# A gated attention unit followed by an MLP mixer: z^T without copies, w_tok2 in its own order, the first u^T on TensorE, x of batch 0 turned later

## The chip, the cores and the metric

One core of one Trainium2 chip runs the whole kernel in one launch. The metric is the time of one execution on the device in microseconds (us), as the median of several runs. TensorE (PE) multiplies, VectorE (DVE) and ScalarE (ACT) work element by element, GpSimd (POOL) copies and issues the casting loads, SyncE (SP) issues the transposing DMAs and the stores. Each engine runs its own instructions in the order in which they were written.

## The reference

There are 8 batches of 3008 rows, 256 channels wide, and z has 64 columns.

```
scores = (z @ z.T) / S;  attn = max(scores, 0) ** 2     # per batch, S = 3008
x  = u * (attn @ v)                                     # 3008 x 256
h  = max(x.T @ w_tok1, 0) @ w_tok2                      # 256 x 3008
u2 = x + h.T
out = u2 + max(u2 @ w_ch1, 0) @ w_ch2
```

w_tok1 is 3008 x 256, w_tok2 256 x 3008, w_ch1 256 x 1536, w_ch2 1536 x 256. All inputs and the output are float32; the kernel multiplies in bf16.

## The kernel before

**Tiles.** Rows of a batch are 24 tiles of 128, the last half full. Four tiles make a group, so a batch has six query blocks q and six key groups g. Rows are loaded so that a partition holds consecutive rows (`rows_of`, L102): within a group, tile t holds rows t, t+4, t+8 and so on. Everything made from z, u and v stands in that order, and w_tok2's columns have to be brought into it.

**Attention.** Scores (L399) multiply z^T with itself over 64 rows, so two key tiles share the array, one on its upper and one on its lower rows. For that zT holds z^T twice, on partitions 0 to 63 and 64 to 127. ScalarE applies max(., 0) out of PSUM into `at` (L437), VectorE squares it (L445), and TensorE multiplies by v into two accumulators (L533). `at` has six buffers. For batches 1 to 7 the score matrix's symmetry is used: a block above the diagonal is turned by a transposing DMA into the block below it (`flip`, L492), and diagonal blocks are filled in the same way (`flip_tiles`, L485). A buffer of `at` that is flipped comes free only when the flip has landed. The first batch computes every block. A finished accumulator is multiplied by u^T (`gate`, L628), which gives x^T; SP turns it into x (`turn_x`, L640).

**Mixer.** When all six blocks of a batch have x, token mixing (L675, L692) and the two channel matmuls (L729, L771) run between the attention work of the next batch. `add` (L698) adds the token-mixed h out of PSUM to x^T.

**z.** For a later batch GpSimd loads a group of z with a cast (`load_z`, L113), copies it twice side by side (`turn_z`, L125), and SP transposes that into four tiles of zT (L126), six times a batch. For batch 0 z is loaded uncast; VectorE doubles and casts it, TensorE turns chunks 0, 1, 4 and 5, and SP turns 2 and 3.

**u.** A block of u is loaded by GpSimd (L179) into one of three buffers and turned by SP (`turn_u`, L189). **w_tok2** is loaded into a staging tile `ws` (L208) and brought into row order by GpSimd copies (L220, L224).

**Order.** The program is written out by a planner (L1000 onwards) that keeps a clock for TensorE, ScalarE, VectorE and SP with fixed costs (`push`), and picks the next piece for TensorE: scores, a half of attn @ v, or a piece of the mixer. Loads and turns are asked for at fixed steps (`at_group`), a step being one key group of one block; batch 0 takes steps 0 to 35. In batch 0 GpSimd's queue loads v of batch 1, w_tok1, w_tok2 and the channel weights from step 7 on. The planner's costs decide only the order; on the chip each engine waits for what it needs.

Of the kernel before, what the change touches and what calls it, by code (L numbers as in the profile page):

```python
# [15 lines left out]
GK = 4  # L16
# [28 lines left out]
class Piece:  # L45


    def __init__(self, cost, needs, fn, opens=False, closes=False, room=None):
        self.cost, self.needs, self.fn = cost, needs, fn
        self.opens, self.closes, self.room = opens, closes, room  # L50


@with_exitstack
def kernel(
# [23 lines left out]
    NG = KT // GK  # L78
    widths = [min(QW, S - q * QW) for q in range(NQ)]
# [15 lines left out]


# [13 lines left out]
    def load_z(b, c):  # L110
        zs = sb.tile([P, GK, d_qk], BF16, tag="zs", name="zs", bufs=6)
        n = full_tiles[c]
        nc.gpsimd.dma_start(out=zs[:, :n, :], in_=rows_of(z[b], c))  # L113
        if n < GK:
            for r in range(2):
                nc.gpsimd.dma_start(
                    out=zs[r * TAIL:(r + 1) * TAIL, n, :], in_=last_rows(z[b]))
        loading(LOAD / 4)
        return zs

    def turn_z(zs, zT, c, engine, tag="zr", bufs=2):


        zr = sb.tile([P, GK, 2, d_qk], BF16, tag=tag, name="zr", bufs=bufs)
        engine.tensor_copy(zr[:], zs.unsqueeze(2).to_broadcast([P, GK, 2, d_qk]))  # L125
        nc.sync.dma_start_transpose(  # L126
            out=zT[:, c * GK:c * GK + GK, :], in_=zr.rearrange("p t h d -> p (t h d)"))
# [77 lines left out]
    def load_w_tok2(c):  # L205
        st = sb.tile([P, DT, QW], BF16, tag="h2", name="ws", bufs=ROOM["h2"])
        W = widths[c]
        nc.gpsimd.dma_start(  # L208
            out=st[:, :, :W],
            in_=moe_w_tok2.rearrange("(tc t) s -> t tc s", t=P)[:, :, c * QW:c * QW + W])  # L210
        ws[c] = st
        live["h2"] += 1
        loading(LOAD)

    def order_w_tok2(c):
        st = ws.pop(c)
        live["h2"] -= 1
        W, n = widths[c], full_tiles[c]
        for h in range(DT):
            nc.gpsimd.tensor_copy(  # L220
                w_tok2_sb[:, h, c * QW:c * QW + n * P].rearrange("p (t s) -> p t s", s=P),
                st[:, h, :n * P].rearrange("p (s t) -> p t s", t=n))
        if n * P < W:
            nc.gpsimd.tensor_copy(  # L224
                w_tok2_sb[:, :, c * QW + n * P:c * QW + W], st[:, :, n * P:W])
# [16 lines left out]
    zTs, vs, urs, uTs, xTs, xs, ws = {}, {}, {}, {}, {}, {}, {}  # L242
# [9 lines left out]

    LAST = NG - 1
# [41 lines left out]

    LOAD = 1.3
# [84 lines left out]
    def score_run(us, start):  # L381
        slots = sorted((d for d in ring if d.t is not None), key=lambda d: d.t)
        for unit in us:
# [12 lines left out]
            for r, i, c0, c1 in parts(unit):  # L396
                k = g * GK + i
                h = slice(r * d_qk, (r + 1) * d_qk)
                nc.tensor.matmul(  # L399
                    sc[:, r, c0:c1], zT[h, k * P:(k + 1) * P],  # L400
                    zT[h, q * QW + c0:q * QW + c1], start=True, stop=True)
# [41 lines left out]
    def square(unit, view, t):  # L443
        (b, q, g), pr = unit
        nc.vector.tensor_mul(view, view, view)  # L445
        if (b, q, g) in early:
            for e in early[b, q, g][2 * pr:2 * pr + 2]:
                e.t = t
            if pr == 0:
                blocks[b, q, g] = (  # L450
                    Done(t), ats[b, q, g].rearrange("p (i w) -> p i w", w=QW), "at", [1])
            else:
                ats.pop((b, q, g))
            return
        if pr < GK // 2 - 1:
            return
        at = ats.pop((b, q, g))
        uses = [1]
        if flips(b, q, g):
            uses[0] = 2  # L460
            attn = at.rearrange("p (j i s) -> p i j s", i=GK, s=P)
            done = push("sp", t, 2.45, 6.5, lambda t: flip(b, q, g, at, uses, done),
                        room=("fl",))
        else:
            attn = at.rearrange("p (i w) -> p i w", w=QW)
        blocks[b, q, g] = (Done(t), attn, "at", uses)

    def square_triangle(unit, t):
# [5 lines left out]
        if pr == 0:  # L474
            for j, busy in ((0, 0.55), (1, 0.4)):
# [3 lines left out]
        done = push("sp", t, 0.3, 5.5, lambda t: blocks.update(  # L479
# [136 lines left out]
    def gate(blk, dh, t):  # L616
# [18 lines left out]
        if dh == DT - 1:  # L635
            push("sp", t, 1.25, 7.5, lambda t: turn_x(b, q, t), first=1)
# [22 lines left out]
    def add_mixer(b):  # L659
# [26 lines left out]
        def tok2(q, end):  # L686
# [9 lines left out]
            def add(t):  # L696
                xT = xTs[b, q]
                nc.vector.tensor_add(xT[:, :, :W], xT[:, :, :W], h[:, :, :W])  # L698
# [187 lines left out]
    def new_zT(b):  # L886
        zTs[b] = sb.tile([P, KT, P], BF16, tag="zT", name="zT", bufs=2)
# [7 lines left out]
    load_v(0, 0)  # L895

# [10 lines left out]
    def turn_next_z(b, c, zs):  # L907
        turn_z(zs, zTs[b + 1], c, nc.gpsimd)
        on_sp(0.6)
        turned[b + 1, c] = Done(pe[0] + 9.0)  # L910
# [7 lines left out]
    for b in range(B):  # L918
# [6 lines left out]
        if b + 1 < B:  # L925
            held = {}

            def ask_z(b, c, held):
                held[c] = load_z(b + 1, c)

            at_group(base + 3 * NG, lambda b=b: new_zT(b + 1))
            for j, c in enumerate(vorder):
                at_group(base + 3 * NG + j, lambda b=b, c=c, h=held: ask_z(b, c, h))
                at_group(base + 3 * NG + j + 3, lambda b=b, c=c, h=held:
                         turn_next_z(b, c, h.pop(c)))
# [3 lines left out]
    def turn_late_z(c):  # L939


        zr = double_first_z(c)
        free["dve"] = max(free["dve"], pe[0]) + 0.45
        while all(d.t is None for d in ring):
            run_engines(next_op()[0][0])
        begin = max(free["dve"] + 0.1, min(d.t for d in ring if d.t is not None))
        take_slot()
        begin, end = on_pe(max(pe[0], begin), "full", 0.23)
        zp = psum.tile([P, GK, P], F32, tag="ps", name="zp", bufs=3)
        turn_on_pe(zr, zp)  # L950
        turned[0, c] = Done()
        ring.append(push(
            "dve", end + 0.1, 0.66, 0.8,
            lambda t: nc.vector.tensor_copy(zTs[0][:, c * GK:c * GK + GK, :], zp[:]),
            first=1, done=turned[0, c]))

    for c in range(GK, NG):
        at_group(c - GK + 1, lambda c=c: turn_late_z(c))
    at_group(3, lambda: turn_u(0, 0))
# [10 lines left out]
    first_tok2 = len(items)  # L970
    items += [lambda c=c: load_w_tok2(c) for c in range(NG)]
    items += [lambda part=part: ask_w_ch(part) for part in range(4)]
    for k, item in enumerate(items):
        n = NG + 1 + k * (NQ * NG - 2 * NG + 4) // len(items)
        at_group(n, item)
        if 0 <= k - first_tok2 < NG:
            at_group(n + 4, lambda c=k - first_tok2: order_w_tok2(c))
# [9 lines left out]
    for c in range(DT, GK):  # L987
        turn_z(zf0[c], zTs[0], c, nc.vector, "h2", 8)
# [5 lines left out]
    score_run(units[:2], 5.3)  # L994

# [4 lines left out]
    while cur[0] is not None or heads or tails:  # L1000
# [32 lines left out]
        if n_now and ts <= t + NOW and (whole or (low and n_now >= 2)):  # L1033
            pick = "scores"
        elif (starved and now and can_score(done_units, now) == now
              and has_turned(units[done_units:done_units + now]) <= t + NOW):
            pick, n_now, ts = "scores", now, t
        elif hold and opened[0] is not None and tm <= t + NOW and pieces is opened[0]:
# [36 lines left out]
        else:  # L1075
            budget -= pieces[0].cost
# [34 lines left out]
```

## Time and profile before

| what | value |
|---|---|
| median of 4 runs | 1177.43 us (1170.79 to 1182.73) |
| the profiled execution | 1178.86 us, span 1176.9 us |
| TensorE matmul busy | 1157.4 us, 98% of the span |
| VectorE, ScalarE, GpSimd busy | 541.0, 521.4, 159.7 us |
| transposes and stores (hardware queue) | 131.74 MB |
| casting loads (software queue) | 32.32 MB written |
| zr copies, GpSimd (L125) | 42, 26.3 us |
| w_tok2 copies, GpSimd (L220, L224) | 13, 10.5 us |
| mean granted TensorE clock | 0.996 |

A line of the profile names the source line, the engine, the operation and its tiles, and then how often and how long. "Idle before" is how long the engine stood before such instructions and what ended it. In the page's rows of 40 digits each digit is a slice of 29.4 us.

### The profile page before, as it was taken

How to read it: one execution, taken by the hardware profiler on the slowest of the kernel's cores; microseconds unless marked ns; L12 is line 12 of the kernel's file. 1: busy time of each engine (PE TensorE's matmuls, PEld its weight loads, DVE VectorE, ACT ScalarE, POOL GpSimd, SP SyncE). 2: the span in 40 equal slices, each digit the busy share in tenths (PEclk: the TensorE clock that was granted, in tenths of full speed). 3: DMA queues.
4: the chain of work that ended last, by engine and by line, in shares of the span. 5: the costliest groups of instructions: out<-in, count | busy, mean ns of one | idle time of the engine just before them, and what ended most of it. 6: DMA issues, size and time to landing. Idle time of an engine off the chain costs nothing.

```text
span 1176.9 us, 17698 instructions
## 1 busy us (share of the span) xinstructions
PE 1157.4 (98%) x6956; PEld 631.2 (54%) x7049; DVE 541.0 (46%) x819; ACT 521.4 (44%) x650; POOL 159.7 (14%) x328
## 2 busy tenths in 40 slices
PE   9997999999999999999999999999999999999998
PEld 3333455655556555465555555555554655555666
DVE  5784652436523464335634354242542436512544
ACT  7885542343633354333533436345353445513221
POOL 4471001002011200110201210011101010000000
PEclk9998999999999999999999999999999999999999
DMA  9999837896578984886859896697676977532121
GB/s 169 184 134 193 160 85 156 167 179 122 134 149 165 170 144 114 161 167 148 156 111 184 154 159 130 126 195 139 126 141 146 192 136 155 124 94 63 50 81 64
DMA packets 472883, 165.57 MB, mean 141 GB/s; under 512 B 436640, under 2 KB 450528, under 8 KB 472800
## 3 DMA queue, kind: packets, MB, share of 16 engines
q1 hardware_dynamic: 444944, 131.74, 53.5%
q0 software_dynamic: 27344, 32.32, 19.5%
q8 instruction: 55, 0.90, 0.3%
q10 hardware_dynamic: 512, 0.38, 0.1%
q14 instruction: 28, 0.23, 0.1%
HBM read 65.40 MB, written 24.64 MB: 77 GB/s over the span
## 4 chain that ended last, share of the span: by engine, by line
PE 95%; DMA 2%; issue 1%; ACT 1%; DVE 1%; SPq 0%; POOL 0%; ACTq 0%; DVEq 0%
PE acc L533 41%; PE op L771 21%; PE hp L729 21%; PE sc L399 6%; PE a_ps L675 4%; PE h_ps L692 3%; DMA fl<-at 1%; ACT at L437 1%; DMA zf<-in_z_dram 1%; DMA v_sb<-in_v_dram 0%; DVE xT L698 0%; DVE at L445 0%; DVE xT L628 0%; DVE h2pre L744 0%; SPq L134 0%
## 5 line engine op out<-in xcount | busy, mean ns | idle before, releaser
L742 ACT ACTIVATE h2pre<-hp 128x1024 bf16<-128x1024 f32 (+1 forms) x191 | 191.0, 1006 | 364.6 <-PE hp L729 363.4
L533 PEld LDWEIGHTS <-v_sb 128*128 128x128 bf16 (+1 forms) x2304 | 209.5, 98 | 266.4 <-issue 65.0
L533 PE MATMUL acc<-at,v_sb 128*128 128x512 bf16 (+2 forms) x1438 | 348.0, 378 | 3.0 <-issue 1.3
L437 ACT ACTIVATE at<-sc 128x1024 bf16<-128x1024 f32 (+1 forms) x284 | 272.0, 1024 | 165.6 <-PE sc L399 155.1
L445 DVE TENSOR_TENSOR at<-at 128x1024 bf16<-128x1024 bf16 (+1 forms) x284 | 199.8, 712 | 183.7 <-ACT at L437 182.8
L729 PE MATMUL hp<-xT,w_ch_sb 128*128 128x512 bf16 (+1 forms) x1115 | 264.8, 374 | 1.9
L771 PE MATMUL op<-w_ch_sb,h2pre 128*128 128x256 bf16 x2208 | 258.4, 273 | 0.3 <-DVE xT L698 0.2
L771 PEld LDWEIGHTS <-h2pre 128*128 128x128 bf16 x2208 | 216.0, 98 | 46.1 <-issue 0.5
L533 PE MATMUL acc<-fl,v_sb 128*128 128x512 bf16 (+1 forms) x819 | 197.6, 370 | 1.4 <-issue 0.5
L729 PEld LDWEIGHTS <-w_ch_sb 128*128 128x128 bf16 x1152 | 112.8, 98 | 126.7 <-issue 0.2
L784 DVE TENSOR_TENSOR res<-op,u_sb 128x512 f32<-128x512 f32 x87 | 60.2, 692 | 206.5 <-PE op L771 206.5
L744 DVE TENSOR_SCALAR h2pre<-hp 128x1024 bf16<-128x1024 f32 (+1 forms) x97 | 117.3, 1209 | 52.4 <-PE hp L729 51.3
L628 DVE TENSOR_TENSOR xT<-acc,uT 128x512 bf16<-128x512 f32 (+1 forms) x96 | 63.3, 665 | 113.7 <-PE acc L533 110.4
L399 PE MATMUL sc<-zT 64*128 64x512 bf16 (+1 forms) x732 | 96.0, 362 | 0.3
L425 ACT ACTIVATE at<-sc 128x512 bf16<-128x512 f32 (+3 forms) x164 | 59.2, 446 | 67.7 <-PE sc L399 67.5
L125 POOL COPY zr<-zs 128x512 bf16<-128x512 bf16 x42 | 26.3, 625 | 401.3 <-DMA zT<-zr 396.3
L473 DVE TENSOR_TENSOR at<-at 128x512 bf16<-128x512 bf16 (+3 forms) x164 | 44.3, 324 | 59.2 <-ACT at L425 59.1
L399 PEld LDWEIGHTS <-zT 64*128 64x128 bf16 x732 | 31.3, 94 | 56.9 <-issue 39.6
L698 DVE TENSOR_TENSOR xT<-xT,h_ps 128x1024 bf16<-128x1024 bf16 (+1 forms) x48 | 55.7, 1193 | 6.4 <-PE h_ps L692 6.3
L675 PE MATMUL a_ps<-x_sb,w_tok_sb 128*128 128x256 bf16 x384 | 47.5, 283 | 5.8 <-ACT at L437 5.8
L675 PEld LDWEIGHTS <-w_tok_sb 128*128 128x128 bf16 x384 | 38.8, 101 | 15.6 <-issue 7.0
L168 POOL DMA_DIRECT2D v_sb<-in_v_dram x48 | 25.9, 546 | 149.5 <-PE acc L533 147.8
(43 smaller groups left out, 217.6 us busy)
## 6 DMA issues: line engine op xcount, KB each, us to landing
out_dram<-res SPq DMA_DIRECT2D x87, 256.0 KB, 2.2
v_sb<-in_v_dram POOLq DMA_DIRECT2D x40, 256.0 KB, 4.7
ur<-in_u_dram POOLq DMA_DIRECT2D x40, 256.0 KB, 5.0
zs<-in_z_dram POOLq DMA_DIRECT2D x35, 64.0 KB, 4.8
at<-at SPq DMA_TRANSPOSE x123, 2.4
fl<-at SPq DMA_TRANSPOSE x105, 4.0
v_sb<-in_v_dram POOLq DMA_DIRECT2D x8, 192.0 KB, 6.3
ur<-in_u_dram POOLq DMA_DIRECT2D x8, 192.0 KB, 5.6
```

What stands on the lines that cost most here:

```text
L399: nc.tensor.matmul(sc[:, r, c0:c1], zT[h, k * P:(k + 1) * P], zT[h, q * QW + c0:q * QW + c1], start=True, stop=True)
L425: nc.scalar.activation(a3[:, i, c0:c1], sc[:, r, c0:c1], ACT.Relu, scale=inv_S)
L437: nc.scalar.activation(view, sv, ACT.Relu, scale=inv_S)
L445: nc.vector.tensor_mul(view, view, view)
L533: nc.tensor.matmul(o, vs[blk.b, g][rows, i, dh * P:(dh + 1) * P], rhs, start=first, stop=stop, skip_group_check=True)
L628: nc.vector.tensor_mul(xT[:, dh, :full * P].rearrange("p (t s) -> p t s", s=P), acc[:, :full * P].rearrange("p (t s) -> p t s", s=P), uT[: ...
L675: nc.tensor.matmul(st["a_ps"][:, th, :], w_tok1_sb[:, k, th * P:(th + 1) * P], x[:, :, i, :], start=(k == 0 and th == 0), stop=(k == KT - ...
L729: nc.tensor.matmul(hp[:, r, :W], w_ch1_sb[:, dc, cc * P:(cc + 1) * P], xT[:, dc, :W], start=(dc == 0), stop=(dc == DT - 1))
L742: nc.scalar.activation(h2[:, :, :W], hp[:, :, :W], ACT.Relu)
L744: nc.vector.tensor_single_scalar(h2[:, :, :W], hp[:, :, :W], 0.0, AX.max)
L771: nc.tensor.matmul(op[:, i, :], h2, w_ch2_sb[:, cc, :], start=(cc == 0 and (i == 0 or apart)), stop=(cc == CHT - 1), skip_group_check=True)
L784: nc.vector.tensor_add(res.rearrange("p i (h d) -> p i h d", d=P), op.rearrange("p i (h d) -> p i h d", d=P), us[:, :, half * 2:half * 2 + ...
```

## The change

- z of a later batch is loaded into one lasting tile `zs` with a zero column block at each end. There is no doubling copy: the transposes read pairs of neighbouring row tiles, once starting at even and once at odd places, so that a tile of zT holds one row tile on its upper and the next on its lower partitions. Scores take the upper half one tile further on (`z_tile`). SP does this for half a batch at a time (two transposes, and one more for the last tile). For batch 1 z is asked for at steps 6 to 11 and turned at 14 and 20, where it had been asked for from step 18 on.
- w_tok2 is loaded straight into place in its natural order; `add` reads h with a step instead.
- The first block of u is turned by TensorE against the identity and copied out by VectorE; z chunks 4 and 5 are turned as urgent pieces as soon as they are expected.
- x of batch 0 is pushed to SP for planned time 62 at the earliest.
- The planner's costs for flips on SP change, and scores are held back a little where the row-split last key tile is about to be ready.

```diff
+    zs = consts.tile([P, KT + 2, d_qk], BF16)
     def load_z(b, c):
-        zs = sb.tile([P, GK, d_qk], BF16, tag="zs", name="zs", bufs=6)
         n = full_tiles[c]
-        nc.gpsimd.dma_start(out=zs[:, :n, :], in_=rows_of(z[b], c))
+        k = c * GK + 1
+        nc.gpsimd.dma_start(out=zs[:, k:k + n, :], in_=rows_of(z[b], c))
...
-    def turn_z(zs, zT, c, engine, tag="zr", bufs=2):
-        zr = sb.tile([P, GK, 2, d_qk], BF16, tag=tag, name="zr", bufs=bufs)
-        engine.tensor_copy(zr[:], zs.unsqueeze(2).to_broadcast([P, GK, 2, d_qk]))
+    def turn_z(zT, half):
+        n = KT // 2
+        for k in (half * n, half * n + 1):
+            nc.sync.dma_start_transpose(
+                out=zT[:, k:k + n:2, :],
+                in_=zs[:, k:k + n, :].rearrange("p t d -> p (t d)"))
+        if half:
+            nc.sync.dma_start_transpose(
+                out=zT[:, KT, :], in_=zs[:, KT:, :].rearrange("p t d -> p (t d)"))
...
+    def z_tile(b, half, k):
+        return k + 1 - half if b else k
...
     def load_w_tok2(c):
-        st = sb.tile([P, DT, QW], BF16, tag="h2", name="ws", bufs=ROOM["h2"])
+        cols = slice(c * QW, c * QW + widths[c])
         nc.gpsimd.dma_start(
-            out=st[:, :, :W],
+            out=w_tok2_sb[:, :, cols],
-    def order_w_tok2(c):
...
-            done = push("sp", t, 2.45, 6.5, lambda t: flip(b, q, g, at, uses, done),
+            done = push("sp", t, 1.8, 6.5, lambda t: flip(b, q, g, at, uses, done),
...
-            for j, busy in ((0, 0.55), (1, 0.4)):
+            for j, busy in ((0, 1.2), (1, 1.2)):
...
-            push("sp", t, 1.25, 7.5, lambda t: turn_x(b, q, t), first=1)
+            push("sp", t if b else max(t, LOADED), 1.25, 7.5,
+                 lambda t: turn_x(b, q, t), first=1)
...
-                nc.vector.tensor_add(xT[:, :, :W], xT[:, :, :W], h[:, :, :W])
+                to = xT[:, :, :n * P].rearrange("p h (t s) -> p h t s", t=n)
+                nc.vector.tensor_add(
+                    to, to, h[:, :, :n * P].rearrange("p h (s t) -> p h t s", t=n))
+                if n * P < W:
+                    to = xT[:, :, n * P:W]
+                    nc.vector.tensor_add(to, to, h[:, :, n * P:W])
...
-            at_group(base + 3 * NG, lambda b=b: new_zT(b + 1))
+            at_group(base + NG, lambda b=b: new_zT(b + 1))
             for j, c in enumerate(vorder):
-                at_group(base + 3 * NG + j, lambda b=b, c=c, h=held: ask_z(b, c, h))
+                ask = base + (NG if b == 0 else 3 * NG - 2)
+                at_group(ask + j, lambda b=b, j=j: load_z(b + 1, j))
+                if j % 3 == 2:
+                    at_group(ask + (2 * j + 4 if b == 0 else j + 3),
+                             lambda b=b, j=j: turn_next_z(b, j // 3))
...
+    def first_u(landed):
+        ur = urs.pop((0, 0))
+        def turn(end):
+            take_slot()
+            up = psum.tile([P, QW // P * DT, P], F32, tag="ps", name="up", bufs=3)
+            for i in range(QW // P * DT):
+                t, h = divmod(i, DT)
+                nc.tensor.matmul(
+                    up[:, i, :], ur[:, t, h * P:(h + 1) * P], ident[:],
+                    start=(i % 4 == 0), stop=True, skip_group_check=True)
+            ring.append(push("dve", end + 0.2, 1.15, 1.3, lambda t: evacuate(up)))
...
+        heads.append(Piece(0.45, [Done(landed)], turn, urgent=True))
...
+        together = (
+            blk is not None and blk.q > 1 and blk.b < B - 1 and not blk.tails
+            and blk.slot == 0 and t + 0.3 < tails_ready(blk) < FAR)
+        if n_now and not together and ts <= t + NOW and (whole or (low and n_now >= 2)):
             pick = "scores"
...
+        elif tm <= t + NOW and pieces[0].urgent:
+            pick = "mixer"
...
+    late_z(4, 7.8)
+    late_z(5, 9.0)
+    first_u(18.5)
```

## The prediction

> **What bounds the kernel now.** I read the page first, then the windows of busy time, then the chain of waits and the queues around the one place where they show a hole.
>
> ```profile
> span 1176.9 us, 17698 instructions
> ...
> PE 1157.4 (98%) x6956; PEld 631.2 (54%) x7049; DVE 541.0 (46%) x819; ACT 521.4 (44%) x650; POOL 159.7 (14%) x328
> ...
> DMA  9999837896578984886859896697676977532121
> ```
>
> TensorE is busy for 98% of the span, VectorE and ScalarE for less than half. Whatever the change takes off GpSimd or VectorE is therefore worth nothing by itself. It pays only where TensorE stands still or is slowed. The DMA engines are full in the first four slices (to about 118 us), while the inputs and weights load, and less full after.
>
> ```profile
> core 0: us, PE busy (x) PEld busy (x) DVE busy (x) ACT busy (x) POOL busy (x), PEclk, DMA share, GB/s
> 10.00:20.00 10.00, 9.07 (x52) 3.21 (x50) 6.68 (x12) 7.09 (x9) 3.86 (x8) 1.00 1.11 197
> 90.00:100.00 10.00, 9.95 (x57) 3.85 (x55) 7.63 (x15) 9.35 (x12) 0.29 (x1) 1.00 1.30 194
> 100.00:110.00 10.00, 5.12 (x26) 1.99 (x25) 0.79 (x4) 0.56 (x3) 2.35 (x5) 0.94 1.15 167
> 110.00:120.00 10.00, 8.65 (x41) 5.08 (x41) 4.78 (x7) 4.67 (x5) 4.06 (x8) 0.54 1.18 223
> 120.00:130.00 10.00, 9.95 (x56) 4.83 (x56) 5.88 (x7) 3.45 (x4) 0.00 (x0) 1.00 1.17 208
> ```
>
> The columns after the stretch are busy time by engine, then the granted clock and the DMA share. Only 100 to 120 us has a hole: TensorE misses 4.88 + 1.35 = 6.2 us, and the clock is at half speed for about 10 us (0.6/0.5 = 1.2 us before 110, 4.6/0.5 = 9.2 us after). TensorE was working again from 110.95 us, so half speed cost it (9.2 - 0.95)/2 = 4.1 us. The hole costs 10.3 us. Later, until the end, TensorE misses 0.4 to 0.7 us in each 100 us.
>
> ```profile
> 98.10 1.03 ACT at L437
> ...
> 100.30 9.47 DMA fl<-at
> ...
> 109.88 0.07 ACT at L437
> ```
> ```profile
> 90.21 1.23 SPq L189 DMA_TRANSPOSE uT<-ur  x1
> 91.68 7.17 SPq L492 DMA_TRANSPOSE fl<-at  x1
> 98.95 1.25 SPq L640 DMA_TRANSPOSE x_sb<-xT  x1
> 100.30 10.75 SPq L492 DMA_TRANSPOSE fl<-at  x3
> ```
>
> The chain, and below it SP's queue, say why. The first flips of batch 1 (fl<-at) go out at 91.7 and 100.3 us and land 9.2 and 9.5 us later; those of 121 to 129 us land every 2 us. ScalarE has no free `at` buffer until a flip lands, so scores stop and then TensorE. SP had itself waited 8.4 us at 90.2 for a load of u, and that first stage's last load landed at 98.5 us.
>
> ```profile
> 49.57 0.70 POOL L208 DMA_DIRECT2D ws<-in_moe_w_tok_dram  x1 [0.72 <-DMA w_tok_sb<-in_moe_w_tok_dram]
> 58.18 0.80 POOL L125 COPY zr<-zs 128x512 bf16<-128x512 bf16 x1 [7.91 <-DMA zT<-zr]
> ...
> 67.48 0.69 POOL L125 COPY zr<-zs 128x512 bf16<-128x512 bf16 x1 [2.55 <-DMA zT<-zr]
> 68.11 2.15 POOL L220 COPY w_tok_sb<-ws 128x512 bf16<-128x512 bf16 x2
> ```
>
> GpSimd's own timeline says why the loads were late: it issues them in order, and its copies wait in that order for z^T transposes. Counting in pieces of 256 KB, the loads issued from 24.5 to 47.2 us, before the copies bite, are 14.9 pieces and are in at 55.3: 2.07 us each, transposes among them included. The next 16 pieces are in at 98.5: 2.7 us each.
>
> **The change, part by part.** *GpSimd's copies.* 42 zr copies (26.3 us) and 13 w_tok2 copies (8.3 + 1.5 + 0.7 us) go: 36.8 us of GpSimd, no time of TensorE by itself. What matters is that no load waits behind them. At 2.07 us a piece, 30.9 pieces from 24.5 us are in at 24.5 + 64 = 88.5 us, 10 us earlier and just ahead of the first flip. GpSimd still waits for u buffers, but by the written order those transposes are early. While the copies ran (66 to 80 us) a 1024-wide square took 1125 ns on VectorE against 694 later; that goes too, hidden as VectorE is.
>
> *z of the next batch.* Five transposes a batch instead of six, 25 tiles instead of 24; a z^T issue takes SP 1.22 us, so SP saves 1.2 us a batch. For batch 1 the eight z loads (about 0.54 us of GpSimd each) move ahead of w_tok1 and between the loads of v, so those come 1.5 pieces, 3 us, later; their first use is past 100 us. On SP a half waits for three to five loads, and behind it stands one u^T that is not needed for a block (14 us). The single `zs` makes GpSimd wait for the transposes of the batch before, a whole batch earlier. What covers all this is distance: none of it is nearer than 10 us to its use. Without it, a late z^T stops scores for as long as it is late.
>
> *z^T's destination is now every second tile.* Triangles already write in such steps: at<-at (one to three tiles) lands in 2.4 us in the median, contiguous u^T (eight tiles) in 3.1. I take no price; the other end is a landing doubled, 3.1 us more for each, still off the path. The Trainium skill, DMA: Bandwidth & Descriptors, "Latency and other measured facts", speaks against this: a transpose with a non-contiguous middle dimension loses some 30% of its rate. By it a batch's z^T would take about 1 us more of DMA and the sum would stay the same; the at<-at landings show no such loss.
>
> *x of batch 0.* Six x_sb transposes stay, but four stand on SP behind u^T of block 5, so they no longer break into the early loads. In 20 to 70 us they landed in 4.2 to 11.7 us, later in 2.8. Behind x of block 3, which waits for its gate at about 66 us, stand u^T of batch 1 and x of block 4; the former is needed at about 105. Price 0; the first user, token mixing, runs past 110 us. [...]
>
> *First u^T on TensorE.* Eight 128-column matmuls: four took 0.40 us (L149), I take 0.45 us net, plus one 1.15 us VectorE evacuation. An added wait: TensorE, with all matmuls behind it, now waits for that load itself (landed 18.8). z chunks 4 and 5 are turned earlier; windows 10 to 30 us miss 0.93 + 0.24 us, 0.9 over the usual. I take -0.9 (bounds 0 and -2; the second v, landed 11.7 us, still holds TensorE; +2 if u is late).
>
> *w_tok2 in natural order.* The reordering moves into 48 adds (L698, 1215 ns), which read PSUM with a stride of four or three; eight get a second piece (0.21 us, as L633). No row shows a strided PSUM read. The low end is 1215 ns; as the high end I double it. GpSimd's reordering copy (863 ns against 625) says 1.38 times; that engine is far off, and I take 1215 since the read is already one element at a time.
>
> *Planner.* Truer costs for flips, and scores held until the row-split tails can join them: in the written orders TensorE changes between half- and full-row matmuls 272 times instead of 280. Six scores need 0.64 us and take 0.75 until the next kind, so 0.11 a change, about -1.0 us.
>
> **Sum**, against the profiled execution (1178.86 us, its span plus 2.0): -10.3 for the hole, -0.9 start, +0.45 u^T, -1.0 changes, and +1.5 because five flips still share the DMAs with u and z of the following loads: 1168.6 us. The median shown is 1177.43 and the runs spread from 1170.79 to 1182.73, about the size of the hole, so I estimate that the hole varies between executions; without it the sum stands for the median too.
>
> **Rivals.** *A: the hole stays.* The loads end late or the following u and z meet the flips, as at 101 us now. For it: my 88.5 us is only 3 us ahead of the flip, and transposes are not fewer. Against: flips need be only some 5 us earlier for TensorE not to stop, and the clock fell 3.8 us after it stopped, so a shorter hole costs half at most. Time: 1178.86 - 0.9 + 0.45 - 1.0 = 1177.4. *B: slower, through the strided adds.* The six adds of a batch run back to back (6.74 us at 1101.6), ahead of channel mixing. Doubled they add 48 x 1.2 = 58 us of VectorE; if half shows, 1168.6 + 29 = 1198. It decides from 0.2 us an add, fully exposed (48 x 0.2 is about the whole gain). Against: the other engines' rows for a half-empty VectorE. At 1.38 times (0.46 us an add, half shown) it is 1179.6. *C: faster still.* The start gains its full 2 us, the +1.5 and u^T's price vanish, and SP's truer costs halve the small later waits (some 5 us in all): 1178.86 - 10.3 - 2.0 - 1.0 - 2.5 = 1163.1. For it: those waits are real; against: no single one is over 0.2 us.
>
> **How the numbers follow.** Forecast 0.58, its own range 1164 to 1173; A 0.18; B 0.14, nearly all slower; C 0.10. Leaving out most of B and the far half of C, 1162 to 1182. No change is within 1% here (1165.7 to 1189.2), about what a measurement tells: faster takes C and a fifth of the forecast, 0.22; slower is B and a rest, 0.15; same 0.63. The likeliest is a gain of 0.75%, on the near side of that bound.
>
> **What would show it.** Right: the window 100 to 120 us with TensorE over 9.8 in each 10 and clock 1.00; flips from 91 us landing in 4 to 6 us; last weight load in by about 88; the add at 1.2 us; 10 to 30 us missing under half a us. Wrong: ScalarE waiting for fl<-at again (A), adds over 1.6 us with matmuls waiting on them (B), or TensorE waiting at the u transpose.

## The result, and the profile after

| | before | changed |
|---|---|---|
| median | 1172.70 us (79 runs, 1169.82 to 1187.55) | 1181.49 us (53 runs, 1169.00 to 1196.05) |
| the profiled execution | 1178.86 us | 1183.68 us |
| ratio to before | | 1.0037, 95% interval 1.0022 to 1.0051 |

The change makes the kernel slower, by 0.4% as the ratio has it. The ratio leaves out runs more than 1.5% above the fastest of their kernel (for the changed kernel above 1186.5 us, 16 of its 53 runs), so the medians, 8.8 us apart, lie further apart than it says. The same program does not always run alike: the mean granted clock is 0.993 in the profiled execution of the changed kernel and 0.998 or more in 11 of its 53 runs (1169.00 to 1175.90 us). A profile therefore shows one execution, here one near the median. The 79 runs of before also correct the four that the prediction started from: half of them are under 1172.7 us, a quarter under 1171.2 us.

The page of the changed kernel, then its windows of busy time (columns as in the prediction):

```profile
span 1181.9 us, 17667 instructions
...
PE 1155.7 (98%) x6964; PEld 631.3 (53%) x7057; DVE 554.3 (47%) x842; ACT 509.1 (43%) x636; POOL 126.5 (11%) x275
...
PEclk9997999999999999999999999999999999999999
```
```profile
10.00:20.00 10.00, 8.56 (x49) 3.34 (x48) 6.96 (x12) 8.11 (x9) 5.16 (x10) 1.00 1.09 189
20.00:30.00 10.00, 9.95 (x61) 3.94 (x61) 8.11 (x13) 8.54 (x10) 3.39 (x7) 1.00 0.81 141
90.00:100.00 10.00, 9.91 (x55) 3.98 (x55) 7.74 (x16) 8.87 (x12) 0.54 (x1) 1.00 1.22 187
100.00:110.00 10.00, 1.58 (x9) 0.50 (x8) 0.65 (x3) 0.36 (x2) 2.64 (x5) 0.75 1.18 158
110.00:120.00 10.00, 6.26 (x32) 3.85 (x32) 2.77 (x4) 3.77 (x4) 0.00 (x0) 0.57 1.02 225
120.00:130.00 10.00, 9.95 (x61) 5.39 (x60) 5.07 (x7) 3.45 (x4) 1.21 (x3) 1.00 0.98 188
```

GpSimd has lost its copies (126.5 us for 159.7), and the hole at 100 to 120 us has not closed but grown: TensorE now misses 8.42 + 3.74 = 12.2 us of these 20, for 6.2 before. The clock is at half for 0.25/0.5 of the first ten (5.0 us) and 0.43/0.5 of the second (8.6 us), 13.6 us in all; TensorE runs again from 113.74 us, so until 118.6 us it works at half speed and loses 2.4 us more. The hole costs 14.6 us where the same working gave 10.3 before. That difference, 4.3 us, is nearly the whole of the 4.8 us between the two profiled executions.

The chain of waits, SP's queue, and the first work of ScalarE and TensorE after the hole:

```profile
98.93 0.61 ACT at L428
...
100.66 2.99 SPq L495
...
103.75 1.25 SPq L645
...
105.10 7.46 DMA fl<-at
...
112.67 1.03 ACT at L440
```
```profile
31.92 10.41 SPq L130 DMA_TRANSPOSE zT<-zs  x2
...
68.00 8.88 SPq L207 DMA_TRANSPOSE uT<-ur  x1
76.93 17.02 SPq L645 DMA_TRANSPOSE x_sb<-xT  x4
...
98.99 4.67 SPq L495 DMA_TRANSPOSE fl<-at  x1
103.75 1.25 SPq L645 DMA_TRANSPOSE x_sb<-xT  x1
105.10 10.99 SPq L495 DMA_TRANSPOSE fl<-at  x4
```
```profile
112.67 3.77 ACT L440 ACTIVATE at<-sc 128x1024 bf16<-128x1024 f32 x4 [12.31 <-DMA fl<-at]
```
```profile
113.74 0.61 PE L402 MATMUL sc<-zT 64*128 64x512 bf16 x2 [12.16 <-ACT at L440]
```

It is the wait of before, ScalarE for an `at` buffer that a flip still holds. But the first flip goes out at 98.99 us, 7.3 us later than before (91.68). The landing that ends the wait is that of the second flip, which stands on SP behind the first and one x: out at 105.10 and in at 112.56 us here, 100.30 and 109.77 before. Ahead of both on SP stand the four x of batch 0, which took 17.0 us to issue, and the last weight load (w_ch) landed at 91.7 us, in the middle of them.

### The profile page after: what moved, and what is told of

It reads as the page before. It is cut to its first block, busy times and chain, and to the rows that moved or that the text cites. A ratio compares the mean times of both kernels' runs of the same rounds, so it can differ in the third digit from the quotient of the medians.

```text
span 1181.9 us, 17667 instructions
## 1 busy us (share of the span) xinstructions
PE 1155.7 (98%) x6964; PEld 631.3 (53%) x7057; DVE 554.3 (47%) x842; ACT 509.1 (43%) x636; POOL 126.5 (11%) x275
## 4 chain that ended last, share of the span: by engine, by line
PE 94%; DMA 3%; issue 1%; DVE 1%; SPq 1%; ACT 0%; POOL 0%; DVEq 0%; ACTq 0%
PE acc L536 41%; PE op L783 21%; PE hp L741 20%; PE sc L402 6%; PE a_ps L680 4%; PE h_ps L697 3%; DMA v_sb<-in_v_dram 1%; DMA u_sb<-xT 1%; DMA fl<-at 1%; DMA zf<-in_z_dram 1%; DVE xT L706 0%; SPq L495 0%; ACT at L440 0%; POOL v_sb L186 0%; SPq L645 0%
## 5 line engine op out<-in xcount | busy, mean ns | idle before, releaser
L536 PE MATMUL acc<-at,v_sb 128*128 128x512 bf16 (+3 forms) x1443 | 348.7, 379 | 3.2 <-DMA v_sb<-in_v_dram 1.3
L754 ACT ACTIVATE h2pre<-hp 128x1024 bf16<-128x1024 f32 (+1 forms) x177 | 177.7, 1006 | 313.9 <-PE hp L741 311.0
L448 DVE TENSOR_TENSOR at<-at 128x1024 bf16<-128x1024 bf16 (+1 forms) x284 | 194.6, 688 | 201.2 <-ACT at L440 200.7
L741 PE MATMUL hp<-xT,w_ch_sb 128*128 128x512 bf16 (+1 forms) x1113 | 261.9, 374 | 2.5 <-DVE xT L706 0.4
L536 PE MATMUL acc<-fl,v_sb 128*128 128x512 bf16 (+1 forms) x817 | 193.1, 370 | 1.4 <-issue 0.5
L756 DVE TENSOR_SCALAR h2pre<-hp 128x1024 bf16<-128x1024 f32 (+1 forms) x111 | 133.7, 1204 | 58.8 <-PE hp L741 58.7
L402 PE MATMUL sc<-zT 64*128 64x512 bf16 (+1 forms) x732 | 95.3, 361 | 12.7 <-ACT at L440 12.2
L197 POOL DMA_DIRECT2D ur<-in_u_dram x48 | 26.0, 544 | 194.9 <-DMA uT<-ur 187.3
L697 PE MATMUL h_ps<-w_tok_sb,a_sb 128*128 128x512 bf16 (+1 forms) x182 | 43.8, 374 | 0.6
```

What stands on the lines that cost most here:

```text
L402: nc.tensor.matmul(sc[:, r, c0:c1], zT[h, k:k + P], zT[h, m + c0:m + c1], start=True, stop=True)
L536: nc.tensor.matmul(o, vs[blk.b, g][rows, i, dh * P:(dh + 1) * P], rhs, start=first, stop=stop, skip_group_check=True)
L697: nc.tensor.matmul(h[:, dh, :W], st["a"][:, th, dh * P:(dh + 1) * P], w_tok2_sb[:, th, q * QW:q * QW + W], start=(th == 0), stop=(th == 1))
L741: nc.tensor.matmul(hp[:, r, :W], w_ch1_sb[:, dc, cc * P:(cc + 1) * P], xT[:, dc, :W], start=(dc == 0), stop=(dc == DT - 1))
L754: nc.scalar.activation(h2[:, :, :W], hp[:, :, :W], ACT.Relu)
L756: nc.vector.tensor_single_scalar(h2[:, :, :W], hp[:, :, :W], 0.0, AX.max)
```

## The experiments

Each was timed in five rounds beside the kernel before, on the same chip, but the sessions were on different chips; so runs of different sessions are compared by their ratio to before, or by their distance from its median. In the diffs "changed" means that the edit is made to the changed kernel.

One thing has to be known before the kernels are compared: an edit can make the planner write another order. By the traces e1, e2, e8, e10 and e12 have the changed kernel's order of work on TensorE and ScalarE. e9 and e13 have another one, the same for both; e3 and e4 have that of before; e5, e6, e7 and e11 differ from the kernel that they were made from.

**1. The two moves on SP and the late loads.** First x of batch 0 back to its early place, then a gate on the loads of the next batch, in the changed kernel and in before: GpSimd copies one element that is ready only when the first block of batch 1 is gated, and its later loads queue behind that.

```diff
# e1 (changed): x of batch 0 as early as it is ready
-    LOADED = 62.0
+    LOADED = 0.0
# e2 (changed) and e3 (before): hold GpSimd's next loads
+    def hold_loads():
...
+        nc.gpsimd.tensor_copy(mark[:, 1:2], xTs[1, 0][:, 0, :1])
...
+    at_group(NQ * NG + NG + 2, hold_loads)
```

> The changed kernel with x of batch 0 pushed to SP as soon as its gate is done (LOADED = 0), all else as changed. Theory 1 (SP's queue: four x transposes stand in a row behind the u^T of block 5, start at 76.9 us while the loads still run, and hold the first flip back to 99.0 us): the first flip goes out at about 91 to 93 us, the hole shrinks to about 6 us of TensorE or less, and the median falls by some 5 us towards the kernel before's 1172.7. Rival 2 (loads that no longer wait behind copies fill the queue, so any transpose takes 10 to 20 us, wherever x stands): the first flip still goes out after 97 us, the hole stays near 12 us and the median near 1181. Rival 3 (strided adds or z^T's stepped destination): no change either, but then the hole is not where the time went.

e1: 1171.33 us (12 runs, 1168.23 to 1191.58), ratio 0.9984 [0.9954, 1.0015]. Its profile has a stop of 2.0 us instead of 12.2 and the clock never falls; the first flip goes out at 90.97 us and the last w_ch load lands at 83.2. So the later x has a part in the loss; a single run at 1191.58 us, with a mean clock of 0.991, suggests that e1 is not free of the hole.

> The changed kernel with GpSimd made to wait for x^T of batch 1, block 0 (one 128x1 copy that reads it) before it issues the u loads of batch 1 from block 3 on and z of batch 2. Theory 4 (these loads, issued at 98.8 to 103 us, meet the first flips and take them from 4 to 7-10 us of landing): the first flip lands within 5 us of its issue instead of 10.5, TensorE's stop shrinks from 12.2 us to 3-6 us, the clock falls for less or not at all, and the median falls by 6 to 12 us, to 1170-1175. Theory 1 alone (the first flip leaves 7 us too late because of SP's queue): the stop shrinks by less than 3 us and the median stays above 1178.

> The kernel before with the same wait ahead of the same loads. Theory 4: its stop of 5.8 us at 105 us goes, every execution is near the floor, 1169 to 1171, and the spread of the runs shrinks to 2 us or so. Theory 1 alone: nothing to gain here, since the first flip already leaves at 91.7 us; median 1172 to 1174 and the same spread up to 1180.

e2: 1178.72 us, 1.0035 [1.0004, 1.0066]; e3: 1173.77 us, 0.9992 [0.9969, 1.0016]. With the following loads held back e2 still has its hole (row of TensorE's waits: total, times, longest):

```profile
PE sc L402 <- ACT at L440: 9.7, 1, 9.7
```

With the loads held back the first flip does land in 3.8 us, for 10.5 in the changed kernel, though it also went out after the last w_ch load (97.8 us); the run does not tell these two causes apart. But it went out only at 102.96 us, behind four x that took 27.7 us to issue, and the stop is 2.5 us shorter, not gone. What is late is the issue.

**2. One part at a time, in before.** e4 loads w_tok2 straight into place and adds with a step; e6 holds x of batch 0 to planned time 62; e7 takes the whole z part (one `zs`, halves, the early place for batch 1) with all else as before.

```diff
# e4 (before)
-            out=st[:, :, :W],
+            out=w_tok2_sb[:, :, cols],
...
-                nc.vector.tensor_add(xT[:, :, :W], xT[:, :, :W], h[:, :, :W])
...
+                nc.vector.tensor_add(
+                    to, to, h[:, :, :n * P].rearrange("p h (s t) -> p h t s", t=n))
...
# e6 (before)
-            push("sp", t, 1.25, 7.5, lambda t: turn_x(b, q, t), first=1)
+            push("sp", t if b else max(t, 62.0), 1.25, 7.5,
+                 lambda t: turn_x(b, q, t), first=1)
# e7 (before)
-                at_group(base + 3 * NG + j, lambda b=b, c=c, h=held: ask_z(b, c, h))
+                ask = base + (NG if b == 0 else 3 * NG - 2)
+                at_group(ask + j, lambda b=b, j=j: load_z(b + 1, j))
...
```

> The kernel before with one part of the change: w_tok2 loaded straight into place and read in a stepped order by the 48 adds; no staging tile, no w_tok2 copies on GpSimd; z as before. Rival 3 (strided adds cost): adds over 1.4 us and the median 3 us or more above before. Theory 2 (copies on GpSimd spaced the loads): w_tok2 and the channel weights are asked for earlier, transposes between 50 and 80 us take over 8 us to land instead of 3 to 7, and the first flip moves by a few us either way; median within 4 us of before. My own estimate: adds at 1.21 us, last load in by 90 instead of 98.5 us, median 1171 to 1174.

e4: 1171.26 us, 0.9988 [0.9968, 1.0008], the last w_ch load in at 88.6 us for 94.1. The w_tok2 part is harmless.

> The kernel before with one line of the change: x of batch 0 pushed to SP for planned time 62 at the earliest. Copies, loads and z stay. Theory 1 (the x move alone makes the loss): the first flip goes out after 95 us, TensorE's stop grows past 6 us and the median rises from 1172 to 1176 or more. Rival 2 (it takes the load queue that the missing copies leave full as well): GpSimd's copies leave room, the x transposes land in 3 to 6 us each, the first flip still leaves by 93 us, and the median stays within 2 us of before.

e6: 1173.14 us, 1.0008 [0.9989, 1.0026]. The x move alone costs nothing that can be measured; its profile has one stop of 2.7 us at 123 us.

> The kernel before with the change's z alone: one lasting tile, transposes of half a batch at stepped places, no zr copies, z of batch 1 asked for at steps 6 to 11; w_tok2 staged and copied as before, x and u as before. If z^T's shape or its early place costs (rival 3): its transposes hold SP for 5 us and more and the first flip leaves after 95 us; median 1176 or more. If not: first flip by 92 us, median 1170 to 1173.

e7: 1176.26 us, 1.0031 [1.0018, 1.0043]. The time is the one that rival 3 gave, but not for its reason: the first flip goes out at 92.91 us, there is no stop at 105 us, and the last w_ch load is in at 81.0. What its profile shows instead is a stop of 5.0 us at 572 us, to which the end of this section comes back.

**3. Both moves turned round.** e5 holds x later still, e9 takes only z of batch 1 back to the later place that the other batches have, e8 does that and takes x back to early, with the two memsets of `zs` behind the first loads; e12 is e8 once more.

```diff
# e5 (changed)
-    LOADED = 62.0
+    LOADED = 95.0
# e9 (changed); e8 and e12 too, with LOADED = 0.0 and the memsets moved
-                ask = base + (NG if b == 0 else 3 * NG - 2)
+                ask = base + 3 * NG - 2
...
-                    at_group(ask + (2 * j + 4 if b == 0 else j + 3),
+                    at_group(ask + j + 3,
```

> The changed kernel with x of batch 0 later still (LOADED = 95): on SP's queue the x transposes now stand behind the first three flips instead of in front of them. Theory 1a (what costs is that a row of x transposes stands in front of the first flip): the first flip goes out at 91 to 95 us, TensorE stops for less than 4 us near 105 us, the median is 1170 to 1175; x lands later, by 112 us, and token mixing may lose 1 to 3 us. Rival 1b (any bunching of x costs, wherever it stands, since the bunch holds up whatever follows it): the fourth and fifth flips come late instead, and the median stays above 1177.

e5: 1187.65 us (4 runs), 1.0133 [1.0116, 1.0150], the slowest of all. Its first flip goes out at 90.36 us, but x transposes stand close together on SP at 103.9 to 114.7 us, ahead of the next flips, and three stops of 4.4, 2.2 and 4.2 us follow, each with a fall of the clock.

> The changed kernel with z of batch 1 asked for and turned at the steps of the other batches (16 to 24), x of batch 0 still held to planned time 62. It fills the fourth corner beside changed (x late, z early), x early with z early, and x early with z late. Theory 1 (the row of x in front of the first flip decides): the first flip leaves after 96 us, TensorE stops for 5 us or more, median 1175 to 1182. Theory 5 (early z alone fills SP's queue, the x row only follows it): the first flip leaves by 92 us and the median is 1169 to 1172.

e9: 1174.70 us, 1.0006 [0.9978, 1.0033]. The hole at 105 us is gone with x still late; the last w_ch load is in at 77.8 us, and the first flips leave early and land soon:

```profile
90.67 3.61 SPq L495 DMA_TRANSPOSE fl<-at  x1
94.39 1.25 SPq L645 DMA_TRANSPOSE x_sb<-xT  x1
95.73 5.79 SPq L495 DMA_TRANSPOSE fl<-at  x3
```

The first landed at 96.63 and the second at 99.78 us. These flips were issued before TensorE's other order could matter to them (it differs from 95.8 us on), so the order does not explain this.

> The changed kernel with x of batch 0 not held back (LOADED = 0), z of batch 1 asked for and turned at the steps of the other batches (16 to 24) instead of 6 to 20, and the two column blocks of zeros written after the first loads are issued. Theory 1 with the start's lesson: the second v lands at 11.7 instead of 12.2 us (0.3 to 0.5 us gained), the first flip leaves by 92 us in nearly every execution, and the median is 1169 to 1170.5, with fewer executions above 1175 than the changed kernel with x early alone. If early z is harmless: the same as that one, 1171.

> The fastest version again, unchanged: x early, z of batch 1 late, zero columns after the first loads. If its freedom from the hole is real: all executions between 1168 and 1170.5, 0.3% below the kernel before. If the five executions of the first time were luck: some above 1173, as with x early alone (three of twelve above 1176).

e8: 1168.50 us (5 runs), 0.9968 [0.9956, 0.9979]; e12: 1170.45 us (12 runs), 0.9958 [0.9928, 0.9987]. This version is faster than both kernels, by 0.3 to 0.4% of before in the ratios and by 3.4 and 2.1 us in the medians. The expectation of e12 was met by half: five of its 12 runs lie above 1170.5 us and one above 1173, but none shows a mean clock under 0.998. Its windows (e8) show the hole closed, and the chip's clock whole:

```profile
100.00:110.00 10.00, 10.00 (x76) 6.42 (x74) 3.24 (x7) 5.49 (x9) 0.00 (x0) 1.00 0.83 183
110.00:120.00 10.00, 10.00 (x51) 4.34 (x50) 8.75 (x10) 2.28 (x4) 3.45 (x7) 1.00 1.17 204
```

In the profiles the two moves are not additive: with z early alone the stop is 2.0 us (e1), with x late alone there is none at 105 us (e9), with both it is 12.2. In the ratios that does not show: e1 and e9, measured from e8 or e12, would add up to 1.0022 or 1.0032, and the changed kernel's 1.0037 has an interval that holds both. In the medians it does: +8.8 us against before for both moves, where the others (-0.9, +2.1, and -3.4 or -2.1 for neither) would add up to 3.3 to 4.6. The ratio leaves the longest runs out, and e9 has the other order and the memsets at their old place.

**4. Do the GpSimd copies help by spacing the loads, and what is u^T on TensorE worth?** e10 stages w_tok2 and copies it on GpSimd as before; e11 is e8 with the first u^T turned by SP.

```diff
# e10 (changed)
-            out=w_tok2_sb[:, :, cols],
+            out=st[:, :, :W],
...
+            at_group(n + 4, lambda c=k - first_tok2: order_w_tok2(c))
# e11 (e8)
+    at_group(3, lambda: turn_u(0, 0))
...
-    first_u(18.5)
```

> The changed kernel with w_tok2 staged and reordered by GpSimd's copies as before; x late and z early as changed. Theory 2 (the missing copies let the loads fill the queue, and only then does the x row hurt): the loads are spaced again, transposes between 55 and 90 us land in 4 to 8 us instead of 13 to 23, the first flip leaves by 94 us, median 1172 to 1175. Theory 1 alone: SP's order is the changed kernel's, so the first flip leaves after 97 us and the median stays at 1178 or above.

e10: 1182.33 us (1168.31 to 1195.55), 1.0044 [0.9999, 1.0088], with a stop of 10.3 us. Neither theory holds whole: the first flip goes out at 90.76 us, as theory 2 had it, but takes 10.9 us to land, and the time is theory 1's. The copies are no help.

> The fastest version so far (x early, z of batch 1 late, zero columns written after the first loads) with the first block of u turned by SP's DMA as before instead of TensorE. If TensorE's turn gains what the prediction said (some 0.5 us net): 0.3 to 1 us slower than that version, with TensorE idle near 23 to 25 us while the first gate waits. If it costs its own 0.45 us and saves nothing: 0.3 to 0.5 us faster.

e11: 1180.72 us, 1.0065 [1.0029, 1.0101], but the planner writes another order with it: stops of 2.1 us at 121 us and 6.5 us at 866 us, far from the first u^T. The run does not price u^T by itself; at its own place it lost 0.5 us (20 to 30 us: TensorE 9.49 for e8's 10.00).

**5. What late x and early z do together.** In the changed kernel the z^T of batch 1 goes out at 31.92 us, behind three u^T and ahead of every x, among the loads of v and z. In e1 an early x (39.14 us) stands ahead of it on SP, and it goes out only at 40.56. The DMA column of the windows (the last: GB/s; the one before: the time that packets took as a share of all engines' time, over 1 when packets overlap) shows what follows, first the changed kernel, then e9:

```profile
30.00:35.00 5.00, 4.95 (x27) 1.84 (x28) 3.39 (x6) 4.43 (x5) 4.09 (x8) 1.00 1.15 149
35.00:40.00 5.00, 5.00 (x29) 1.88 (x29) 3.81 (x7) 4.00 (x5) 1.06 (x2) 1.00 1.29 97
40.00:45.00 5.00, 4.84 (x26) 1.89 (x25) 3.19 (x5) 4.19 (x5) 1.06 (x2) 1.00 1.70 74
45.00:50.00 5.00, 5.00 (x29) 1.95 (x29) 2.95 (x5) 4.24 (x6) 1.25 (x3) 1.00 1.32 92
```
```profile
30.00:35.00 5.00, 4.95 (x29) 1.81 (x27) 3.39 (x6) 4.03 (x6) 2.07 (x4) 1.00 1.11 182
35.00:40.00 5.00, 5.00 (x28) 1.91 (x25) 3.81 (x7) 4.41 (x5) 2.12 (x4) 1.00 1.15 201
40.00:45.00 5.00, 4.84 (x28) 1.92 (x29) 2.96 (x6) 4.12 (x5) 3.10 (x7) 1.00 1.23 202
45.00:50.00 5.00, 5.00 (x30) 1.93 (x26) 3.13 (x5) 4.32 (x5) 2.88 (x6) 1.00 1.33 164
```

The DMA engines are just as busy, and move less than half: (97 + 74 + 92) x 5 us = 1.3 MB from 35 to 50 us, for 2.8 MB. At e9's 200 GB/s the missing 1.5 MB are, by my estimate, some 8 of the 14 us by which the last w_ch load is later; where the rest was lost was not taken apart. The last run separates the transposes from the small z loads: z of batch 1 is loaded as early as in the changed kernel, x is as late, and only the z^T are issued later.

```diff
# e13 (changed)
-                    at_group(ask + (2 * j + 4 if b == 0 else j + 3),
+                    at_group(base + 3 * NG + 1 + j,
```

> The changed kernel with one edit: z of batch 1 is still loaded early (steps 6 to 11, among the loads of v), but its z^T transposes go to SP at the later steps 21 and 24 instead of 14 and 20; x of batch 0 stays held to planned time 62. In the changed kernel the core's DMA moved 97, 74 and 92 GB/s in the three 5 us windows from 35 to 50 us, with its engines busy all the time; with the whole z part late it moved 201, 202 and 164. Theory T: it is the four z^T transposes issued at 32 to 55 us, landing after 18 to 23 us, that choke the loads. Then here the windows from 35 to 45 us come back to 180 GB/s or more, the last w_ch load lands by about 80 us instead of 91.7, the first flip goes out by about 91 instead of 99.0, no hole at 105 us, and the time falls to 1170 to 1176. Rival L: the small z loads themselves, eight of them at 64 KB or less between the loads of v, choke the queue. Then the windows from 35 to 45 us stay under 130 GB/s, the hole stays, and the time stays at 1179 to 1184. Rival S: neither; the x row on SP holds the flip whatever the loads do: the windows come back but the first flip still goes out after 96 us.

e13: 1177.10 us (12 runs, 1173.30 to 1184.04), 1.0046 [1.0024, 1.0069]. Its windows and SP's queue:

```profile
35.00:40.00 5.00, 5.00 (x29) 1.95 (x26) 3.80 (x7) 4.41 (x5) 1.08 (x3) 1.00 1.30 150
40.00:45.00 5.00, 4.84 (x28) 1.95 (x29) 2.96 (x6) 4.04 (x5) 3.99 (x9) 1.00 1.12 210
45.00:50.00 5.00, 5.00 (x28) 1.90 (x25) 3.13 (x5) 4.40 (x5) 2.44 (x4) 1.00 1.19 200
...
100.00:110.00 10.00, 9.95 (x71) 5.54 (x68) 6.28 (x12) 7.24 (x10) 2.54 (x6) 1.00 1.11 231
```
```profile
44.72 10.29 SPq L130 DMA_TRANSPOSE zT<-zs  x2
...
90.59 5.09 SPq L495 DMA_TRANSPOSE fl<-at  x1
```

The loads come back (but for 150 GB/s at 35 to 40 us, which is less than expected: the small z loads or the u^T beside them take a part), the last w_ch load lands at 77.5 us, the flip goes out at 90.59, and there is no hole. In this execution theory T holds for the loads and the flips. (The other order helps a little: the second flip lands at 101.79 us, and in the changed kernel's order, where TensorE runs out of work at 101.58, that would be a stop of some 1.4 us.) The time does not follow: 1177.10 us is outside theory T's range, and by the ratio e13 is no better than the changed kernel. The profile is of its fastest run (1173.30 us, mean clock 0.998); the others have 0.994 to 0.998, and what they wait for was not seen. By their traces e13 and e9 differ only in where the eight z loads stand, and e9 is at 1.0006 with no run above 1176.67 us. So the early z loads seem to have a price of their own, as rival L had it, though the two intervals overlap.

Over the profiles with the changed z part, one execution each, the split is clean (e12 and e11 have the loads as in e8):

| | first z^T out, us | GB/s at 35-40, 40-45, 45-50 us | last w_ch load in, us | first flip out, in, us | second flip out, in, us | longest stop of TensorE at 95 to 115 us |
|---|---|---|---|---|---|---|
| changed | 31.92 | 97, 74, 92 | 91.7 | 98.99, 109.49 | 105.10, 112.56 | 12.2 |
| e2 | 30.61 | 104, 117, 189 | 97.8 | 102.96, 106.79 | 106.05, 109.95 | 9.7 |
| e5 | 30.20 | 108, 94, 185 | 94.1 | 90.36, 100.29 | 95.66, 104.04 | 4.4 |
| e10 | 31.76 | 112, 76, 183 | 96.8 | 90.76, 101.67 | 100.93, 110.38 | 10.3 |
| e1 | 40.56 | 120, 206, 178 | 83.2 | 90.97, 99.72 | 96.71, 102.27 | 2.0 |
| e7 | 42.17 | 137, 209, 191 | 81.0 | 92.91, 98.26 | 95.97, 100.81 | none |
| e9 | 43.28 | 201, 202, 164 | 77.8 | 90.67, 96.63 | 95.73, 99.78 | none |
| e13 | 44.72 | 150, 210, 200 | 77.5 | 90.59, 99.20 | 97.12, 101.79 | none |
| e8 | 54.13 | 207, 199, 160 | 77.4 | 90.94, 96.70 | 95.96, 99.91 | none |

In every row with a stop TensorE goes on 1.2 us after the second flip has landed (112.56 and 113.74 us in the changed kernel). With z^T issued near 31 us the loads end 14 to 20 us later than in e9 (in e10 the copies have a part in it), and then either x holds SP until both flips are late (changed, e2) or the first goes out in time, while the last loads still run, and the two take 8 to 11 us each to land (e5, e10); in e10 the first also holds SP for 8.7 us. e2, e5 and e10 have the early z loads and the late x too, so the table by itself does not part z^T from them; e13 (early z loads, late x, later z^T) and e1 (early z loads, early x) do.

**A second place.** e7, e9, e11 and e13 lose 3.7 to 6.5 us in one stop at 572 or some 860 us. The rows of e13, first its waits of TensorE, then VectorE, then SP:

```profile
PE sc L402 <- DVE res L796: 3.7, 1, 3.7
```
```profile
858.16 0.69 DVE L796 TENSOR_TENSOR res<-op,u_sb 128x512 f32<-128x512 f32 x1 [5.68 <-DMA u_sb<-xT]
```
```profile
850.80 2.36 SPq L720 DMA_TRANSPOSE u_sb<-xT  x1
```

TensorE waits for VectorE's `res`, and that for the transpose into u_sb that went out at 850.80 us and landed 7.3 us later, behind loads of the next blocks' z, u and v issued from 845.7 to 848.7 us (213 GB/s at 850 to 855 us). e9 and e13, which share an order, both have it at some 855 us, and e8, in the changed kernel's order, has none there; what in the order brings it about was not taken apart. It is part of why e9 and e13 stay behind e8.

## Why the prediction was wrong, point by point

**The hole, -10.3 us.** Its place and its chain were read rightly, and twice misjudged in value. The profiled execution of before (1178.86 us) was one of its slowest (70 of its 79 runs are no longer), and its mean clock of 0.996 is low: of the 110 runs of before beside e1, e5, e9 and e13, 81 have 0.998 or more. So, by their clock, most of its executions have a smaller hole or none, and against the median e8 and e12 gain 0.3 to 0.4% in the ratio, 3.4 and 2.1 us. And the change did not remove it.

**The step that failed** is, under "z of the next batch", "What covers all this is distance: none of it is nearer than 10 us to its use." I priced the eight loads as 3 us of delay and the transposes by the time until they are needed. Neither is the price: it lies on the loads that the early transposes run among, which at 35 to 50 us move 1.3 MB instead of 2.8. The sum took 2.07 us a piece from the rows of before as if it stayed the same with the work rearranged. The last weight load, expected "by about 88", was in at 91.7 us (94.1 before; the 98.5 us of the prediction is a load of u). With z^T later it is 77.4 to 77.8, better than I worked out: with the w_tok2 copies gone alone it was 88.6 (e4), with the zr copies gone 81.0 (e7).

**x of batch 0, price 0.** True in the kernel before (e6: 1.0008), false in company: 1.0037 for the changed kernel and 0.9984 with x early (e1). I looked at what stands behind x on SP late in the stage (u^T, with 10 us to spare) and not at what had stood behind it early: z^T, which moved up to 31.9 us. Then, loads still running, four x took 17.0 us to issue where e9 issued one in 6.5 us and three in 8.3 us, and the first flip behind them came 7 to 8 us late. e8, the best, has x early. For z^T amid the v and z loads the runs show a price: with z^T early the last load is in at 91.7 us, with z^T alone later at 77.5 (e13).

**Start, -0.9 us.** It is +0.3: TensorE is busy 8.56 + 9.95 us in 10 to 30 us, for 9.07 + 9.76 before. The two memsets of `zs` put the first loads 0.25 us back and the second v landed at 12.16 us for 11.68. I had counted GpSimd's copies and not its new memsets. With these moved, and z late, e8 has 9.03 + 10.00; that is 0.2 us better than before, not 0.9.

**Sizes that held.** The strided add, on which rival B stood:

```profile
L706 DVE TENSOR_TENSOR xT<-xT,h_ps 128x1024 bf16<-128x1024 bf16 x40 | 47.1, 1214 | 0.7 <-PE h_ps L697 0.6
L706 DVE TENSOR_TENSOR xT<-xT,h_ps 128x768 bf16<-128x768 bf16 x8 | 7.6, 948 | 0.0
L710 DVE TENSOR_TENSOR xT<-xT,h_ps 128x128 bf16<-128x128 bf16 x8 | 2.2, 280 | 0.0
L990 DVE CAST uT<-up 128x1024 bf16<-128x1024 f32 x1 | 1.2, 1225 | 0.1
L983 PE MATMUL up<-ident,ur 128*128 128x128 bf16 x8 | 0.6, 219 | 0.0
```

1214 ns for the whole blocks, as L698 before: a step of four cost nothing here, and B is false. The extra piece takes 0.28 us for my 0.21. u^T's eight matmuls are 0.6 us busy and its evacuation 1.2, as taken. z^T into every second tile lands in 2.8 us in the median over the run (3.5 before, for other pieces): no sign of a doubled landing, though a smaller loss cannot be told from pieces of other sizes (nor could it from the at<-at landings that the prediction leaned on, of one to three tiles against eight). The squares of VectorE that took 1125 ns beside the copies take 691 at 66 to 80 us. The small terms together are what can be read from e8's profiled 1168.98 us: 0.4 us over the profiled time of before less its hole (1168.6), where my four summed to 0.05. The -1.0 for fewer row changes was not separated.

**The rivals.** A, "the hole stays", was the right one (I gave it 0.18), and what was to show it came: ScalarE waiting for fl<-at again. But I let it cost no more than the hole of before; nothing in my working allowed the hole to grow. My forecast of 1168.6 us lies near the times of e8 and e12 (1168.50 and 1170.45), two runs of a kernel that is not this change; since the start, the hole and the load time in its sum were each off, that it lies so near is luck.

## What to carry to other kernels

Before moving transposes to an earlier place, look at which loads are then in flight: their price can fall on the loads, and with it on the first use of all that queues behind, and not on the transpose's own use. On an in-order queue a moved item has two effects, on what it is put ahead of and on what it no longer holds back; work out both, and test moves in pairs, since here neither move alone opened the hole in its profile. Compare the written orders too: an edit to one queue can reorder all the others. And before spending a profile's hole as a gain, ask how slow the profiled execution was among its kernel's runs.

## What the runs showed of the hardware

**Busy DMA engines are no measure of bytes.** At 40 to 45 us the changed kernel has a share of 1.70 and moves 74 GB/s; e9 moves 202 at 1.23. Long landings of the transposes are not the sign of it: in e8 the first z^T landed after 18.3 us too, among the w_tok and w_ch loads, and these went on at about 200 GB/s (50 to 70 us). The profiles that choke have z^T issued near 31 us among the loads of v and the smaller ones of z (8 KB of z issued at 33.15 us landed 15.6 us later). z loads beside them are not enough: e9's first two z^T went out at 43.28 and 45.57 us among loads of z, and the rate stayed at 202 and 164 GB/s. Why these and not the others is open.

**The half clock lasts in steps.** Worked out from the granted clock in the windows: 3.4 us after stops of 3.7 (e13) and 5.0 us (e7), 6.8 after 4.5 (e9) and 6.5 (e11), 10.2 to 10.4 after 5.8 (before), 9.7 (e2) and 10.3 (e10), 13.6 after 12.2 (changed). Short stops cost a step too: 3.4 us after 2.1 (e11, at 121 us), 2.7 (e6) and 3.0 (e3), but none after 2.0 (e1). The Trainium skill, TensorE: Matmul & The Clock Gate, Part 1, gives a free-running window of 3413 ns; the steps agree with multiples of it, and stops of 5.0, 6.5 and 5.8 us cost one, two and three of them.
